# Token sums and reciprocals moved behind two groups of the output projection, and a third side unit moved ahead of the attention output

## The chip, the cores and the metric

The kernel runs on one core of one Trainium2 chip. Its time is the device time of that core in microseconds (us). A comparison goes by the median of several runs of each kernel on the same chip. Beside the timed runs there is one execution that the hardware profiler recorded; busy times, waits and starts of single instructions come from it.

## The reference

The inputs are a sequence of 2048 tokens of width 512, cut into 64 segments of 32 tokens, and a memory of 8 rows. Two branches are mixed by a gate for each token:

```
g = sigmoid((x * gate_w).sum(-1))
out = g * A(x) + (1 - g) * B(x)

A: for each segment s, in order
   h = [mem (8 rows), segment (32 rows)]
   q, k, v = h @ Wq, h @ Wk, h @ Wv          # 32 heads of width 128
   p = softmax(q k^T * scale, masked)        # memory columns are always open
   o = (p v) @ Wo
   mem = o[:8]                               # needed by the next segment
   result rows = o[8:]
B: layernorm -> @ w1 -> gelu -> @ w2
```

The 64 segments form a chain: the memory that segment s hands over is 8 rows of its output projection, and nothing of q, k and v of segment s+1 is complete without it. Branch B does not depend on the chain.

## The kernel before

**Stages.** A first stage of about 80 us computes branch B for part of the tokens and loads the four weight matrices. Then a loop of 64 steps follows, one for each segment. The kernel writes out the order of every engine's instructions by hand (`tc.manual_schedule()`), so the order in the source is the order on each engine. `T, si = divmod(s, 4)`: four segments make one tile of 128 tokens.

**The 32 columns of a step.** A step works on 8 memory rows and 24 of its own 32 tokens. The last 8 tokens of each segment ("left" tokens) are collected for a whole tile. Their q, k, v (`left_qk`, `left_v`) and their output projection (`wo_left`) are computed as filling work, called side units here: generators, from which `run(n)` takes the next n units. One unit is four matmuls with 512 moving columns each, which run side by side on four column tiles of TensorE (in tile 15 it is eight matmuls of 256 columns of branch B). `side(T, si)` picks the generator, and `WS` says how many units are taken at three places: `W1` before the attention output, `W2` between it and the output projection, `W3` after the projection.

**One step on TensorE, in order.**
1. `qk_unit` (L128): q and k of the step, 16 groups of four matmuls. ScalarE casts each bank (L133), VectorE transposes it into `QT` and `KT` (L137).
2. `scores(s, 0)` (L266, L270) for the first half of the heads, then v of the first half (`v_unit`, L147) and the first quarter of the second.
3. `xsums(E, 0)` (L702): the sums of the exponentials over the keys for the token queries, as eight tiny matmuls (4 moving columns, the exponentials as weights) into eight columns `xs8` of the bank `SbF`. Then `msum(0)` (L277, L280): the same for the memory queries, which `mnorm(0)` (L799, L800 on VectorE) turns into normalised weights in `E`.
4. `scores(s, 1)`, the rest of v, `msum(1)` and `mnorm(1)`, and two halves of a matmul unit of branch B (L675). `v_cast` (L809) copies v to SBUF on ScalarE.
5. `run(W1)`, then `xsums(E, 1)` and `recip_x(s)`.
6. `av` (L290, L295): the attention output of all heads, on four row tiles, first for heads of the first half and then of the second. The second half needs the result of `mnorm(1)`.
7. ScalarE copies the memory columns to `UT` (L840, four copies) and the token columns unnormalised to `XR` (L708, `x_raw`). Meanwhile `run(W2)`.
8. `wo_pass` (L159): the output projection as 8 groups of four matmuls of 512 columns into bank `X2`. The weights are `UT`: 8 memory columns of this step and 24 token columns of the step before, so the tokens lag one step.
9. `new_mem` (L747): the 8 memory rows are transposed into `hT` of the next step, with units of `W3` between.

**The token normalisation.** `recip_x` takes the reciprocal of `xs8` on VectorE (L713), stores it to DRAM (`r_dr`, L716 on the SP queue), issues the next load of `hm` (L654), and reads `r_dr` back as `Rb`, the same values on all partitions (L719, 512 KB written). VectorE then copies two results (L721) and writes the mask for the next step into `SbF`, which also clears `xs8` (`mask_put(0)`, L259); GpSimd adds to `racc` (L723). In the next step `x_norm` (L731) multiplies `XR` by `Rb` on GpSimd: two operations into `UT`, two into `UL`. `wo_pass` of that next step reads this `UT`. `prep_q` (L249) and `prep_h` (L245) stand in GpSimd's queue as well.

The lines that the change touches, with their surroundings:

Of the kernel before, what the change touches and what calls it, by code (L numbers as in the profile page):

```python
# [28 lines left out]
def kernel(ctx, tc, A_x, A_mem0, A_Wq, A_Wk, A_Wv, A_Wo, A_seg_len, B_x, B_w1, B_b1, B_w2, B_b2, gate_w, out):  # L29
    nc = tc.nc  # L30
    P = 128
    _, S, Dm = A_x.shape
# [80 lines left out]
    X2 = lps.tile([P, 512], FP32)  # L113
    SbF = lps.tile([P, 512], FP32)
    W = lps.tile([P, 512], FP32)
# [39 lines left out]
    def wo_group(bk, U_, n):  # L155
        j, ih = HORD[n]
        for c in range(4):
            i = 4 * ih + c
            nc.tensor.matmul(bk[32 * c:32 * c + 32, :], lhsT=U_[:, j, i, :], rhs=Wo_sb[:, 4 * i + j, :],  # L159
                             start=(n == 0), stop=(n == NW - 1), tile_position=(0, 32 * c))  # L160
# [6 lines left out]
    def flush(q, n=1):  # L167
        for _ in range(min(n, len(q))):
            q.pop(0)()
# [73 lines left out]
    def prep_h(s):  # L243
        T, si = divmod(s, SPT)
        nc.gpsimd.tensor_copy(out=hT[s % 3][:, :, 0:RIDE], in_=xTs[T][:, :, seg * si:seg * si + RIDE])  # L245
# [11 lines left out]
    def mask_put(i2):  # L257
        c = 4 * EW + (NG + 2 * M if i2 == 0 else 0)
        nc.vector.tensor_copy(out=(SbF, U[0])[i2][:, 0:c], in_=MkF[:, 0:c])  # L259
# [346 lines left out]
    UT = [lp.tile([P, 4, NG, 32], BF16, name=f"UT{i}") for i in range(2)]  # L606
# [22 lines left out]
    def side(T, si):  # L629
        gens = []  # L630
        if si == 2:
            gens = [wo_left(T - 1, X1) if T >= 1 else mlp_units(8)]
        elif T + 1 == NT:
            gens = [mlp_units(4)] if si < 2 else []
        else:
            gens = [[left_qk(T + 1, 0, 0, X1), left_qk(T + 1, 1, 0, U[3])], [left_qk(T + 1, 0, 1, X1), left_qk(T + 1, 1, 1, U[3])], [],
                    [left_v(T + 1, 0, X1), left_v(T + 1, 1, U[3])]][si]
        return chain(*gens)
# [10 lines left out]
    def hm_load(n):  # L649
        for _ in range(n):  # L650
            if work:
                T, fc = work.pop(0)
                hm = cw.tile([P, P], BF16, tag="hm", bufs=5, name="hm")
                nc.sync.dma_start(hm[:], h_dr[T][fc])  # L654
                hms.append((T, fc, hm, 1))
# [42 lines left out]
    def xsums(E, h):  # L698

        for c0, n in ((8, 32), (0, LEFT)):  # L700
            for c in range(4):
                nc.tensor.matmul(xs8[32 * c:32 * c + n, 4 * h:4 * h + 4], lhsT=E[:, 4 * h + c, c0:c0 + n], rhs=BO[:, 0:P:32],  # L702
                                 start=False, stop=True, skip_group_check=True, tile_position=(0, 32 * c))
# [7 lines left out]
    def recip_x(s):  # L711
        R = Rs.pop(s)
        nc.vector.reciprocal(out=R[:, 8 * NG:RW], in_=xs8)  # L713

        Rb = cw.tile([P, P, NG], FP32, tag="Rb", bufs=1, name="Rb")
        nc.sync.dma_start(r_dr[s % 2][:], R[:, 8 * NG:RW])  # L716
        hm_load(owed[0])
        owed[0] = 0
        nc.sync.dma_start(Rb[:].rearrange("p r e -> p (r e)"), r_dr[s % 2][:].rearrange("r e -> (r e)").partition_broadcast(P))  # L719
        for i2 in (1, 0):  # L720
            nc.vector.tensor_copy(out=R[:, 32 * i2:32 * i2 + 32], in_=RP[i2])  # L721
        mask_put(0)
        nc.gpsimd.tensor_tensor(out=racc[:, 0:RW], in0=racc[:, 0:RW], in1=R[:, 0:RW], op=ALU.add)  # L723
        Rbs[s] = Rb

    def x_norm(s):
        T, si = divmod(s, SPT)
        XR, Rb = XRs.pop(s), Rbs.pop(s)[:].rearrange("p (c q) (h j) -> p h j c q", c=4, h=2)
        for out, o, a, b in ((UT[(s + 1) % 2], M, LEFT, 32), (UL[T % 2], LEFT * si, 0, LEFT)):
            for h in range(2):  # L730
                nc.gpsimd.tensor_tensor(out=out[:, :, 4 * h:4 * h + 4, o:o + b - a], in0=XR[:, :, 4 * h:4 * h + 4, a:b], in1=Rb[:, h, :, :, a:b], op=ALU.mult)  # L731

    def wo_pass(U_, cuts=(0, Dm), bk=W):
        for n in range(NW):
            wo_group(bk, U_, n)
        w = cw.tile([P, Dm], BF16, tag="w", bufs=8, name="w")
        for a, b in zip(cuts, cuts[1:]):
            nc.scalar.copy(out=w[:, a:b], in_=bk[:, a:b])  # L738
        return w
# [9 lines left out]
        nc.vector.tensor_copy(out=hn[:, k0:k0 + nk, RIDE:32], in_=bk.rearrange("p (k m) -> p k m", k=nk))  # L749


    WS = ((2, 2, 1), (2, 2, 2), (2, 2, 2), (2, 2, 2))
    for s in range(nseg):
        T, si = divmod(s, SPT)
        last = s == nseg - 1
        hc, hn = hT[s % 3], hT[(s + 1) % 3]
        W1, W2, W3 = WS[si]
        fill = side(T, si)
        if s + 1 < nseg:
            prep_h(s + 1)  # L760
        if s >= 1:
            x_norm(s - 1)
        if si == 0 and T >= 2:
            c_load(T - 2)
        if si < 3:
            vp_load(T, si + 1)
        if last:
            c_load(T - 1)
            c_load(T)
        if si == 0 and T + 2 < NT:  # L770
            load_xT(T + 2)
        if s in (2, (NT - 1) * SPT):
            hm_load4()
        for n, (t, hf) in enumerate(((0, 0), (1, 0), (0, 1), (1, 1))):
            bk = U[n]
            for kc in range(KC):
                qk_unit(bk, hc, t, hf, kc)
            if n == 0:
                flush(act_q, 9)
                flush(dve_q, 9)  # L780
            qk_tr(qk_cast(bk[:]), (QT, KT)[t], hf, LEFT * (1 - t))
            if n == 0:
                mask_put(1)
        V = cw.tile([P, NG, Dh], BF16, tag="V", name="V")
        E = cw.tile([P, NG, EW], BF16, tag="E", name="E")
        R = cw.tile([P, NG * 40], FP32, tag="R", name="R")
        Rs[s] = R
        xsum = SbF[:, 0:32 * NG].rearrange("p (i q) -> p i q", q=32)

        def exps(i2, x):  # L790
            c = slice(0, 40) if x else slice(40, EW)
            nc.scalar.activation(out=E[:, 4 * i2:4 * i2 + 4, c], in_=Sb[i2][:, :, c], func=ACTF.Exp, scale=scale)  # L792

        def msum(i2):
            sums(U[1 + 2 * i2][:, 320:352].rearrange("p (i q) -> p i q", q=8), E[:, 4 * i2:4 * i2 + 4, :], 40, 48, 8, True)

        def mnorm(i2):
            r, e = RP[i2], E[:, 4 * i2:4 * i2 + 4, 40:56].rearrange("p i (a q) -> p i a q", q=8)
            nc.vector.reciprocal(out=r, in_=U[1 + 2 * i2][:, 320:352])  # L799
            nc.vector.tensor_tensor(out=e, in0=e, in1=r.rearrange("p (i q) -> p i q", q=8).unsqueeze(2).to_broadcast([P, 4, 2, 8]), op=ALU.mult)  # L800

        scores(s, 0)
        nc.scalar.activation(out=E[:, 0:4, :], in_=Sb[0], func=ACTF.Exp, scale=scale)
        for kc in range(KC):
            v_unit(X1, hc, 0, kc)

        def v_cast(vb, h):
            i0 = 4 * vb + 2 * h
            nc.scalar.copy(out=V[:, i0:i0 + 2, :].rearrange("p i e -> p (i e)"), in_=(X1, X2)[vb][:, 256 * h:256 * h + 256])  # L809

        v_cast(0, 0)
        v_unit(X2, hc, 1, 0)
        if not last:
            xsums(E, 0)
            msum(0)
            mnorm(0)
        scores(s, 1)
        exps(1, 0)
        v_cast(0, 1)
        exps(1, 1)  # L820
        for kc in range(1, KC - 1):
            v_unit(X2, hc, 1, kc)
        if not last:
            if s:
                next(mlp, None)
            msum(1)
            mnorm(1)
        v_unit(X2, hc, 1, KC - 1)
        for h in range(2):
            v_cast(1, h)  # L830
        if last:
            break
        run(W1)
        if s:
            next(mlp, None)
        xsums(E, 1)
        recip_x(s)
        av(s, V, E)
        for j in (0, 2, 1, 3):
            nc.scalar.copy(out=UT[s % 2][:, j, :, 0:M], in_=U[j][:, 0:NG * 40].rearrange("p (i q) -> p i q", q=40)[:, :, 32:40])  # L840
        x_raw(s)
        run(W2)
        prep_q(s + 1)
        w = wo_pass(UT[s % 2], (0, P, 2 * P, Dm), X2)
        if s >= 1:
            ws[s - 1] = w
        run(W3)
        for _ in extra(T, si):
            pass
        new_mem(w, hn, 0)  # L850
        run(1)
        new_mem(w, hn, 1)
        run(1)
        new_mem(w, hn, 2)
        for _ in fill:
            pass
        if si == 3 and T + 2 < NT:
            left_x(T + 2)
        flush(dve_q, 9)
        nc.vector.tensor_tensor(out=rmin[:, 0:RW], in0=rmin[:, 0:RW], in1=R[:, 0:RW], op=ALU.min)  # L860
        flush(act_q, 9)
# [174 lines left out]
```

## Time and profile before

| what | value |
|---|---|
| median of 3 runs | 759.48 us (759.0 to 761.15) |
| the profiled execution, its own time | 762.61 us |
| its span | 760.8 us, TensorE clock 0.999 |
| TensorE matmul busy | 741.7 us, 97% |
| ScalarE busy | 537.2 us, 71% |
| VectorE busy | 400.5 us, 53% |
| GpSimd busy | 274.7 us, 36% |

In the rows of the trace the engines are PE (TensorE matmuls), PEld (its weight loads), DVE (VectorE), ACT (ScalarE), POOL (GpSimd) and SPq (the queue of SyncE that issues DMAs). A row of the timeline gives start, duration, engine, line, operation, tiles with their shapes, and in brackets the idle time of the engine before it with what ended it. Consecutive instructions of one kind are merged (x8), and their duration is then from the first start to the last end. A matmul's duration contains the way through the array, so the distance between the starts of two groups is the better measure of what a group costs: the groups of four 512-column matmuls follow each other every 0.21 us, though one is listed with 0.38 us. For the same reason a TensorE that is busy 97% of the time is not without waits.

### The profile page before, as it was taken

Reading aid. Unit: us, or ns where it says so; the run is one execution under the profiler, and the core shown is the slowest. Engines: PE = TensorE matmul, PEld = TensorE weight load, DVE = VectorE, ACT = ScalarE, POOL = GpSimd, SP = SyncE. Lnnn points to the kernel's source line nnn. Section 1 sums busy time; section 2 is a strip of 40 time slices with the busy share of each in tenths; the row PEclk is TensorE's granted clock in tenths of the full one; section 3 lists DMA queues with packets and bytes.
Section 4 is the critical chain, followed back from the end, with each engine's and each line's share of the span. In section 5 each row is a group of like instructions: output and inputs, shape, how many; then the busy total and the mean of one; then the engine's idle time right before and its main releaser. Section 6 shows DMA issues by size and latency. Waiting matters only on the chain.

```text
span 760.8 us, 44957 instructions
## 1 busy us (share of the span) xinstructions
PE 741.7 (97%) x19710; PEld 422.9 (56%) x19710; DVE 400.5 (53%) x1415; ACT 537.2 (71%) x1626; POOL 274.7 (36%) x517
## 2 busy tenths in 40 slices
PE   8999999999999999999999999999999999999996
PEld 4776455555555555555555556555555555555553
DVE  5767545545445545446454555444454545545454
ACT  5767666777777777777777777677777777777663
POOL 4001234433344342443434443424433344442441
PEclk9999999999999999999999999999999999999999
DMA  9999522232222323122222213232222212222221
GB/s 308 324 319 332 136 75 60 69 83 78 66 64 72 94 66 90 59 74 76 80 80 63 87 47 99 66 86 56 73 77 90 79 61 72 61 87 73 85 69 45
DMA packets 74971, 75.70 MB, mean 99 GB/s; under 512 B 42377, under 2 KB 64882, under 8 KB 73234
## 3 DMA queue, kind: packets, MB, share of 16 engines
q1 hardware_dynamic: 73730, 71.07, 30.9%
q8 instruction: 156, 2.56, 1.4%
q0 software_dynamic: 496, 1.18, 0.5%
q10 hardware_dynamic: 544, 0.52, 0.2%
q14 instruction: 45, 0.37, 0.2%
HBM read 59.49 MB, written 6.98 MB: 87 GB/s over the span
## 4 chain that ended last, share of the span: by engine, by line
PE 86%; issue 1%; DVE 1%; ACT 0%; DVEq 0%; POOL 0%
PE U L128 33%; PE X L159 18%; PE X L147 16%; PE X L128 4%; PE U L290 3%; PE W L675 2%; PE U L147 2%; PE U L266 1%; PE U L747 1%; PE SbF L266 1%; PE U L295 1%; PE SbF L702 1%; PE U L277 1%; PE W L159 0%; PE U L280 0%
## 5 line engine op out<-in xcount | busy, mean ns | idle before, releaser
L731 POOL TENSOR_TENSOR UT<-XR,Rb 128x384 bf16<-128x384 bf16 x126 | 140.1, 1134 | 309.2 <-DMA Rb<-r_dr 261.2
L133 ACT CAST Tb<-U 128x512 bf16<-128x512 f32 x288 | 168.9, 587 | 81.6 <-PE U L128 79.0
L128 PEld LDWEIGHTS <-hT 128*32 128x32 bf16 x4096 | 107.8, 96 | 100.3 <-DVE hT L749 8.1
L147 PE MATMUL X<-Wv_sb,hT 128*32 128x512 bf16 x2048 | 144.6, 378 | 0.5 <-issue 0.5
L128 PE MATMUL U<-Wq_sb,hT 128*32 128x512 bf16 x2048 | 136.5, 381 | 0.2 <-DVE hT L749 0.2
L128 PE MATMUL U<-Wk_sb,hT 128*32 128x512 bf16 x2048 | 133.2, 379 | 0.0
L159 PE MATMUL X<-Wo_sb,UT 128*32 128x512 bf16 x2016 | 121.0, 380 | 0.2 <-issue 0.2
L749 DVE CAST hT<-U 128x8 bf16<-128x8 f32 x126 | 21.0, 167 | 167.6 <-PE U L747 126.5
L809 ACT CAST V<-X 128x256 bf16<-128x256 f32 x256 | 88.7, 372 | 15.7 <-PE X L147 5.0
L137 DVE STREAM_TRANSPOSE QT<-Tb 128x256 f32<-128x256 f32 x128 | 56.6, 442 | 73.7 <-ACT Tb L133 73.0
L159 PEld LDWEIGHTS <-UT 128*32 128x32 bf16 x2080 | 57.1, 96 | 56.1 <-issue 14.0
L708 ACT CAST XR<-U 128x256 bf16<-128x256 f32 x252 | 78.3, 432 | 0.0
L738 ACT CAST w<-X 128x128 bf16<-128x128 f32 x189 | 44.7, 309 | 44.8 <-PE X L159 44.8
L137 DVE STREAM_TRANSPOSE KT<-Tb 128x256 f32<-128x256 f32 x128 | 56.9, 445 | 30.9 <-ACT Tb L133 23.2
L731 POOL TENSOR_TENSOR UL<-XR,Rb 128x128 bf16<-128x128 bf16 x126 | 60.3, 501 | 0.0
L147 PEld LDWEIGHTS <-hT 128*32 128x32 bf16 x2048 | 47.1, 95 | 21.6 <-issue 1.0
L840 ACT CAST UT<-U 128x64 bf16<-128x64 f32 x252 | 35.9, 225 | 28.3 <-PE U L295 28.3
L723 POOL TENSOR_TENSOR racc<-racc,R 128x72 f32<-128x72 f32 x63 | 21.2, 337 | 94.7 <-DVE R L721 81.8
L792 ACT ACTIVATE E<-U 128x64 bf16<-128x64 f32 (+1 forms) x128 | 35.0, 273 | 11.4 <-PE U L270 10.8
L480 PEld LDWEIGHTS <-w_sb 128*128 128x128 bf16 (+1 forms) x352 | 33.5, 100 | 15.2 <-issue 2.4
L747 PEld LDWEIGHTS <-w 128*32 128x32 bf16 x1008 | 23.6, 93 | 31.9 <-ACT w L738 25.2
L128 PE MATMUL X<-Wq_sb,GL 128*32 128x512 bf16 x496 | 38.7, 381 | 1.3 <-issue 1.2
(173 smaller groups left out, 1237.8 us busy)
## 6 DMA issues: line engine op xcount, KB each, us to landing
Rb<-r_dr SPq DMA_DIRECT2D x63, 512.0 KB, 4.0
Wv_sb<-in_A_Wv_dram SPq DMA_DIRECT2D x4, 1024.0 KB, 6.5
Wq_sb<-in_A_Wq_dram SPq DMA_DIRECT2D x4, 1024.0 KB, 8.5
Wk_sb<-in_A_Wk_dram SPq DMA_DIRECT2D x4, 1024.0 KB, 8.5
Wo_sb<-in_A_Wo_dram SPq DMA_DIRECT2D x4, 1024.0 KB, 11.3
VP<-VL SPq DMA_DIRECT2D x64, 64.0 KB, 3.5
hm<-h_dr SPq DMA_DIRECT2D x69, 32.0 KB, 2.0
c<-c_dr SPq DMA_DIRECT2D x16, 128.0 KB, 3.5
```

The lines of the kernel that those rows point to most:

```text
L128: nc.tensor.matmul(bk[32 * j:32 * j + 32, :], lhsT=G[:, kc, :], rhs=W5[t][:, kc, h0:h1, j, :], start=(kc == 0), stop=(kc == KC - 1), tile_ ...
L133: nc.scalar.copy(out=Tb[:], in_=bk.rearrange("p (a b e) -> p a e b", a=8, b=2))
L137: nc.vector.transpose(out=dst[:, 8 * hf:8 * hf + 8, c0:c0 + 32, :].rearrange("p a r b -> p a (r b)").bitcast(FP32), in_=Tb[:].rearrange("p ...
L147: nc.tensor.matmul(bk[32 * j:32 * j + 32, :], lhsT=G[:, kc, :], rhs=Wv5[:, kc, 4 * vb:4 * vb + 4, j, :], start=(kc == 0), stop=(kc == KC - ...
L159: nc.tensor.matmul(bk[32 * c:32 * c + 32, :], lhsT=U_[:, j, i, :], rhs=Wo_sb[:, 4 * i + j, :], start=(n == 0), stop=(n == NW - 1), tile_po ...
L480: nc.tensor.matmul(hp[:rows, 0:TB * P], lhsT=w1_sb[:, kc, fc * P:fc * P + rows], rhs=yTs[blk][:, kc, :], start=(kc == 0), stop=(kc == KC - 1))
L708: nc.scalar.copy(out=XR[:, j], in_=U[j][:, 0:NG * 40].rearrange("p (i q) -> p i q", q=40)[:, :, 0:32])
L731: nc.gpsimd.tensor_tensor(out=out[:, :, 4 * h:4 * h + 4, o:o + b - a], in0=XR[:, :, 4 * h:4 * h + 4, a:b], in1=Rb[:, h, :, :, a:b], op=ALU ...
L738: nc.scalar.copy(out=w[:, a:b], in_=bk[:, a:b])
L792: nc.scalar.activation(out=E[:, 4 * i2:4 * i2 + 4, c], in_=Sb[i2][:, :, c], func=ACTF.Exp, scale=scale)
L809: nc.scalar.copy(out=V[:, i0:i0 + 2, :].rearrange("p i e -> p (i e)"), in_=(X1, X2)[vb][:, 256 * h:256 * h + 256])
L840: nc.scalar.copy(out=UT[s % 2][:, j, :, 0:M], in_=U[j][:, 0:NG * 40].rearrange("p (i q) -> p i q", q=40)[:, :, 32:40])
```

## The change

Three edits. The two `xsums` calls and `recip_x` leave their places before `av` and are handed to `wo_pass` as a function `mid`, which is called after the second of its eight groups; so both `xsums` run there one after the other, 16 tiny matmuls, followed by all that `recip_x` issues. `WS` takes three side units before the attention output and one after it, in place of two and two; the number after the projection stays. On VectorE, ScalarE and the SP queue the order of instructions stays as it was, apart from single places in the last tile; on GpSimd `prep_q` now stands before the addition to `racc`.

```diff
-    def wo_pass(U_, cuts=(0, Dm), bk=W):
+    def wo_pass(U_, cuts=(0, Dm), bk=W, mid=None):
         for n in range(NW):
             wo_group(bk, U_, n)
+            if n == 1 and mid:
+                mid()
@@
-    WS = ((2, 2, 1), (2, 2, 2), (2, 2, 2), (2, 2, 2))
+    WS = ((3, 1, 1), (3, 1, 2), (3, 1, 2), (3, 1, 2))
@@
         if not last:
-            xsums(E, 0)
             msum(0)
             mnorm(0)
@@
         run(W1)
         if s:
             next(mlp, None)
-        xsums(E, 1)
-        recip_x(s)
         av(s, V, E)
...
         run(W2)
         prep_q(s + 1)
-        w = wo_pass(UT[s % 2], (0, P, 2 * P, Dm), X2)
+
+        def token_sums():
+            for h in range(2):
+                xsums(E, h)
+            recip_x(s)
+
+        w = wo_pass(UT[s % 2], (0, P, 2 * P, Dm), X2, token_sums)
```

## The prediction

> **What bounds the kernel now.** I read the page's head and the groups first, then how regular the steps are, then the timeline of one undisturbed step around the moved work, and last the steps that are longer.
>
> ```profile
> span 760.8 us, 44957 instructions
> PE 741.7 (97%) x19710; PEld 422.9 (56%) x19710; DVE 400.5 (53%) x1415; ACT 537.2 (71%) x1626; POOL 274.7 (36%) x517
> ...
> PE 86%; issue 1%; DVE 1%; ACT 0%; DVEq 0%; POOL 0%
> ```
>
> TensorE bounds the whole span, and no single wait stands out. So the change can win or lose only in the small waits of a step. The reciprocal of the token sums (L713) runs once a step, so its starts give the length of steps:
>
> ```profile
> L713 DVE RECIPROCAL R<-SbF x63: 195/208/208, 87.5 to 738.1; 128x8 f32<-128x8 f32 x63
> ...
> 360.86 0.21 DVE L713 RECIPROCAL R<-SbF 128x8 f32<-128x8 f32 x1 [0.21 <-PE SbF L702]
> 371.09 0.21 DVE L713 RECIPROCAL R<-SbF 128x8 f32<-128x8 f32 x1 [0.22 <-PE SbF L702]
> ...
> 423.08 0.21 DVE L713 RECIPROCAL R<-SbF 128x8 f32<-128x8 f32 x1 [0.21 <-PE SbF L702]
> 433.54 0.21 DVE L713 RECIPROCAL R<-SbF 128x8 f32<-128x8 f32 x1 [0.21 <-PE SbF L702]
> ```
>
> A clean step takes 371.09 - 360.86 = 10.23 us; where `out_sel` runs as well (14 steps) it takes 10.46. From 87.5 to 738.1 are 62 steps, 650.6 us. Clean they would take 62 x 10.23 + 14 x 0.23 = 637.5. So 13.1 us are irregular waits, and the rest is a fixed chain that repeats. I take it apart in the step around 412 us:
>
> ```profile
> 410.47 0.45 DVE L137 STREAM_TRANSPOSE KT<-Tb 128x256 f32<-128x256 f32 x1 [0.36 <-ACT Tb L133]
> 410.83 0.20 PE L702 MATMUL SbF<-BO,E 128*32 128x4 bf16 x8
> 410.89 0.18 PE L277 MATMUL U<-E,BO 128*32 128x32 bf16 x4
> 410.96 0.18 PEld L266 LDWEIGHTS <-KT 128*32 128x32 bf16 x16
> ...
> 411.93 0.61 PE L147 MATMUL X<-Wv_sb,GL 128*32 128x512 bf16 x8
> 412.16 0.65 ACT L809 CAST V<-X 128x256 bf16<-128x256 f32 x2
> 412.36 0.29 PE L675 MATMUL W<-w_sb,hm 128*32 128x256 bf16 x4
> 412.41 0.23 DVE L800 TENSOR_TENSOR E<-E,RS 128x64 bf16<-128x64 bf16 x1
> 412.47 0.22 PE L702 MATMUL SbF<-BO,E 128*32 128x4 bf16 x8
> 412.62 0.27 PE L290 MATMUL U<-E,V 32*128 32x40 bf16 x16
> 412.76 0.32 PE L290 MATMUL U<-E,V 32*128 32x40 bf16 x16
> 412.85 0.21 DVE L713 RECIPROCAL R<-SbF 128x8 f32<-128x8 f32 x1 [0.22 <-PE SbF L702]
> 412.93 0.19 PE L295 MATMUL U<-E,VP 32*128 32x64 bf16 x4
> 413.05 0.62 PE L147 MATMUL X<-Wv_sb,GL 128*32 128x512 bf16 x8
> 413.15 0.56 ACT L840 CAST UT<-U 128x64 bf16<-128x64 f32 x4 [0.35 <-PE U L295]
> 413.48 0.15 PEld L159 LDWEIGHTS <-UT 128*32 128x32 bf16 x8 [0.31 <-issue]
> 413.51 0.40 PE L159 MATMUL X<-Wo_sb,UT 128*32 128x512 bf16 x4
> ```
>
> Two things are to be seen. The second scores load `KT` at 410.96, 0.04 us after its transpose ends (410.47 + 0.45): their start belongs to VectorE. And after the attention output's last group (412.93) two side units run from 413.05 on, and two take 0.43 (411.93 to 412.36, where the next work starts), so until 413.48; the projection's weights load at 413.48, after the ScalarE copy that started at 413.15 and that a wait of 0.31 us on the load queue stands for. Two units cover the copy of `UT` almost exactly, with nothing to spare.
>
> **The change part by part.** The sum is made against the profiled execution, 762.6 us, which lies 3.1 above the median of the runs shown, 759.5; the difference is carried over to that median. The moved work issues in 63 steps.
>
> *Side unit ahead of the attention output.* A unit costs 0.43/2, rounded 0.21 us of TensorE. Put before `av`, it delays all that follows by that. Behind `av` nothing is saved: the first projection group starts 413.51 - 412.93 = 0.58 us after `av`'s last group whatever stands between, since L295, then the copy L840, then the weight load is the chain. With one unit TensorE is done at about 413.26 on this step's clock and waits 0.25. The cover that was used there is gone, and what is late next is the projection and with it the new memory. Bounds: 0 (if something before `av` held TensorE that long) and +0.21; the rows from 411 on show full groups up to 412.36, so +0.21.
>
> *`xsums(E, 1)` out of the place before `av`.* Between L675 and `av` lie 0.26 us now (412.36 to 412.62): 0.11 for 256 columns, 0.06 for the eight tiny matmuls, 0.09 for the change from column to row tiles, which stays. Bounds 0 and -0.06; I take -0.04.
>
> *Waits within `av`.* Its second half waits for `v_cast`, which ends at 412.81 (412.16 + 0.65). With `av` 0.17 later this wait goes. From 412.76 to 412.93 are 0.17, and the first half takes 0.14 for as many matmuls: bounds 0 and -0.04, and I take -0.025.
>
> *`xsums(E, 0)` out of the place before `msum(0)`.* The eight cost 0.06 us there (410.83 to 410.89), but what follows waits for `KT` at 410.96 anyway. Gain: 0. Only the wait grows.
>
> *Both inside the projection.* 16 tiny matmuls between groups of 512 columns, at the 0.06 for eight just read: +0.11 (bounds 0.06, if the first eight hide behind the group ahead, and 0.20, with a bubble like the 0.09 above). Nothing hides it: the copies of `w`, `new_mem` and the next step's q hang on the projection's last group.
>
> *What `recip_x` issues.* L713, two L721 and L259 take 0.8 us on VectorE (412.85 to 413.65) and would end some 1.2 us before the copies for `hT` that stand behind them: 0. The store, the load of `hm` and the load of `Rb` keep their order on SP; `hm` has several tiles in flight: 0. On GpSimd `racc` and `prep_q` swap places: 0.
>
> Fixed part: 0.21 - 0.04 - 0.025 + 0.11 = +0.26 us a step, times 63 = **+16.4 us**.
>
> *The token normalisation comes later.* L713 now follows `av` (0.28), the gap (0.58), two groups (0.43) and the way from the first sum to VectorE (0.38 for eight, 412.47 to 412.85, and 0.06 for the others): 1.7 us after `av`'s start against 0.23 now, 1.5 later. The chain behind it:
>
> ```profile
> 391.79 0.21 DVE L713 RECIPROCAL R<-SbF 128x8 f32<-128x8 f32 x1 [0.22 <-PE SbF L702]
> 398.92 1.13 POOL L731 TENSOR_TENSOR UT<-XR,Rb 128x384 bf16<-128x384 bf16 x1 [5.72 <-ACT Tb L133]
> 401.11 0.95 POOL L731 TENSOR_TENSOR UL<-XR,Rb 128x128 bf16<-128x128 bf16 x2
> 401.58 0.56 DVE L800 TENSOR_TENSOR E<-E,RS 128x64 bf16<-128x64 bf16 x1
> 401.80 0.27 PE L290 MATMUL U<-E,V 32*128 32x40 bf16 x16
> 402.07 0.20 DVE L713 RECIPROCAL R<-SbF 128x8 f32<-128x8 f32 x1
> 402.20 0.28 PE L290 MATMUL U<-E,V 32*128 32x40 bf16 x16
> 407.48 1.13 POOL L731 TENSOR_TENSOR UT<-XR,Rb 128x384 bf16<-128x384 bf16 x1 [4.03 <-DMA Rb<-r_dr]
> ...
> L800 DVE TENSOR_TENSOR E<-E,RS x63: 224/226/893, 87.2 to 737.8; 128x64 bf16<-128x64 bf16 x63
> ```
>
> `x_norm` starts 5.4 us (402.07 to 407.48) to 7.1 us (391.79 to 398.92) after L713 and occupies GpSimd for 3.1 us. While it does, the L800 with both inputs in SBUF (`E`, `RS`) is held: it took 0.56 us and ended at 402.14, after GpSimd's 402.06, and `av`'s second half came 0.40 after the first instead of 0.14. Its longest is 0.893 against 0.226. Counted from `av`'s start, `x_norm` now runs from 5.6-7.3 to 8.8-10.5, and L800 comes at 10.0, so only the latest collide, and I put them at 1.5 us in all. Afterwards `x_norm` runs from 7.1-8.8 to 10.2-11.9 and L800 comes at 10.1: nearly every step collides. L800 gained 0.17 of slack from the side unit and has about 0.4 in all, so the short operations on `UL` (0.5) hardly matter; one on `UT` (1.13) leaves 0 to 0.7. Some 45% of the steps fall there (`x_norm` starting after 7.9), at a mean of 0.22: 63 x 0.45 x 0.22 = 6.2, and 1.1 for the few steps where the DMA is so late that the projection waits for `UT`. Against 1.5 now: **+5.8 us** (bounds -1.5 and +9).
>
> The Trainium skill, "SBUF — State Buffer", section "SBUF: two separate sides", says that VectorE with two SBUF inputs and GpSimd take a port pair exclusively for a whole instruction; it speaks against moving GpSimd's work onto L800, and the trace agrees, with 0.893 against 0.226.
>
> *The irregular waits.* The 13.1 us less 1.5 leave about 11.6 in steps like this one:
>
> ```profile
> PE U L295 <- issue: 3.1, 6, 0.8
> ...
> 210.66:213.62 2.96, 2.96 (x138) 1.95 (x131) 1.83 (x7) 2.43 (x8) 1.52 (x3) 1.00 0.36 76
> 205.30:210.66 5.36, 5.36 (x133) 2.68 (x128) 2.14 (x8) 3.57 (x9) 1.64 (x2) 1.00 0.47 137
> ...
> 213.61 0.19 PE L295 MATMUL U<-E,VP 32*128 32x64 bf16 x2
> 214.64 0.20 PE L295 MATMUL U<-E,VP 32*128 32x64 bf16 x2 [0.84 <-issue]
> ...
> q8 instruction: 156, 2.56, 1.4%
> ```
>
> TensorE stops in the middle of four like matmuls, with no semaphore. Queue q8 brings instructions in pieces of 2.56 MB / 156 = 16 KB, about 256 of TensorE's 39420 loads and matmuls (128 pairs). Six such stops fall on L295 alone (the waits' row), others close by; they come every third step, when a block that starts near the first scores ends at `av`: its 128 pairs (138 with those over the edges) ran in 2.96 us, against 5.36 for the block before, which ended without a stop. The next piece, I infer, is there only some 3.5 to 4 us after the last. The change takes 32 rows of tiny sums out of that stretch and puts 8 of a side unit in, so the same block ends 24 rows further, behind `av`, the remaining unit, the wait for `UT` and two groups of the projection. That is about 0.9 us later, as much as the longest of these stops. I leave 2 of the 11.6 us: **-9.6 us** (bounds 0 and -11.6).
>
> The Trainium skill, "Runtime: NRT & Kernel Launch", section "Instruction fetch mechanics", has blocks of 256 instructions too, but calls the crossing mostly hidden. By that there would be nothing to win here; the 0.84 us of idle before 214.64 says otherwise, and the measurement decides.
>
> Sum: 16.4 + 5.8 - 9.6 = +12.6 us; 762.6 becomes 775.2, and at the runs' median 759.5 + 12.6 = **772 us**, slower by 1.7%. A difference within 0.3% (2.3 us) can't be told from no change.
>
> **The rivals.**
> - *Faster: the side unit falls into a wait.* If the head of `av` is held by `mnorm(1)` or `v_cast` for 0.21 us or more a step, the unit is free. Then 772 - 63 x 0.21 = 759, and without collisions 753. For it: the second half of `av` does wait for `v_cast`. Against: it does so by less than 0.06, and `av`'s first matmul follows the last tiny sum by no more than the change of tiles takes. It decides from 0.20 us of wait a step on (12.6/63). 6%.
> - *Collisions in every step.* If L800 meets the first half of a `UT` operation each time, as in its longest case, `av` waits 0.45 us more: 63 x 0.45 = 28 in place of 7.3, 793 us. For it: the windows overlap in nearly all steps. Against: the DMA's time scatters by 1.7 us. 8%.
> - *No collisions*, because VectorE gets in between two operations or `Rb` lands sooner: 772 - 7.3 = 765. 18%.
> - *The instruction blocks go on stopping TensorE*, at another place: 772 + 9.6 = 782. For it: as many instructions in a step as before, and 16 tiny ones in one place make a new fast stretch. Against: it is followed and preceded by groups of 0.21 us for eight rows. 12%. If the 11.6 us come from something else than the blocks, nothing is won either, and the time is the same. By the page of the Trainium skill named last ("Runtime: NRT & Kernel Launch", "Instruction fetch mechanics") it would come out so.
>
> **How the numbers follow.** My forecast has 56%; with it, the rival without collisions and the one at 782 it is slower by over 0.3%, and so is the 793. Slower: 56 + 18 + 12 + 8 = 94, less 4 that I keep for an edit mispriced in the fixed part: 90%. Of these 4 and the 6 of the first rival, 7 are faster and 3 within 0.3%. The range goes from 764 (no collisions, the stops gone wholly) to 782 (the stops unchanged).
>
> **What the profile after would show.** PEld's wait before the first L159 of a step grows to about 0.5 us, and one group of L147 or L128 lies between L295 and L159. A clean step takes 10.49 us. L266's second load stays 0.04 us behind `KT`'s transpose. The median of L800 on `RS` rises well above 226 ns, with `x_norm` ending near or behind `av`'s start. Idle of TensorE put down to "issue" around L295 falls. Wrong would be: a clean step of 10.3 or less, or the first L159 within 0.4 us of the last L295.

## The result and the profile after

The changed kernel takes 782.27 us (median of 4 runs, 781.26 to 783.25), the kernel before 759.24 (median of 4, 758.42 to 761.15): a ratio of 1.0294, 95% interval 1.0271 to 1.0318. It is slower, as forecast, by 23.0 us where 12.6 were forecast, and it lies 0.3 us above the range's upper end. The profiled execution of after took 783.25 us, 1.0 above its median; that of before lay 3.4 above its own. So 2.4 of the 23.0 us don't stand between the two traces, whose spans differ by 20.6 us.

The page's head and the shares of the chain, after:

```profile
span 781.4 us, 44943 instructions
PE 756.4 (97%) x19710; PEld 422.9 (54%) x19710; DVE 417.1 (53%) x1415; ACT 536.6 (69%) x1626; POOL 273.6 (35%) x517
...
PE 84%; DVE 5%; DMA 4%; ACT 3%; issue 2%; POOL 1%; SPq 0%; DVEq 0%; POOLq 0%; ACTq 0%
```

TensorE has as many instructions as before. VectorE's busy time grew by 16.6 us (400.5 to 417.1) with as many instructions, and its share of the chain went from 1% to 5%: the first sign of an operation that is held. A clean step, in the timeline:

```profile
369.15 0.28 PE L290 MATMUL U<-E,V 32*128 32x40 bf16 x16
...
377.33 0.45 DVE L137 STREAM_TRANSPOSE KT<-Tb 128x256 f32<-128x256 f32 x1 [0.36 <-ACT Tb L133]
...
377.83 0.17 PEld L266 LDWEIGHTS <-KT 128*32 128x32 bf16 x16
...
379.65 0.27 PE L290 MATMUL U<-E,V 32*128 32x40 bf16 x16
379.79 0.28 PE L290 MATMUL U<-E,V 32*128 32x40 bf16 x16
379.89 0.22 PE L295 MATMUL U<-E,VP 32*128 32x64 bf16 x4
380.05 0.40 PE L147 MATMUL X<-Wv_sb,GL 128*32 128x512 bf16 x4
380.17 0.56 ACT L839 CAST UT<-U 128x64 bf16<-128x64 f32 x4 [0.52 <-PE U L295]
380.50 0.24 PEld L159 LDWEIGHTS <-UT 128*32 128x32 bf16 x8 [0.35 <-issue]
380.53 0.62 PE L159 MATMUL X<-Wo_sb,UT 128*32 128x512 bf16 x8
380.96 0.27 PE L702 MATMUL SbF<-BO,E 128*32 128x4 bf16 x16
381.04 0.57 PEld L159 LDWEIGHTS <-UT 128*32 128x32 bf16 x16
381.38 0.21 DVE L713 RECIPROCAL R<-SbF 128x8 f32<-128x8 f32 x1 [1.79 <-PE SbF L702]
```

From one `av` to the next are 379.65 - 369.15 = 10.50 us; 10.49 was forecast, against 10.23 before. The second scores' weights load 0.05 us after `KT`'s transpose ends (377.83 against 377.78). One group lies between L295 and the projection, and the projection starts 0.64 us after L295's last group, as long as before to within 0.06: TensorE waits for the copy of `UT` instead of covering it.

The waits of TensorE and of its loads (sum in us, times, longest); all but the second are new or have grown:

```profile
PEld L290 <- issue: 17.8, 56, 0.6
PEld L159 <- issue: 15.4, 45, 0.3
PEld L290 <- DVE E L802: 7.7, 24, 0.4
PEld L159 <- POOL UT L731: 3.7, 8, 1.0
PEld L675 <- DMA hm<-h_dr: 2.5, 1, 2.5
PEld L159 <- POOL UL L871: 1.9, 1, 1.9
...
PE U L290 <- DVE E L802: 3.0, 10, 0.5
```

L802 is the old L800, which finishes `mnorm`. The 17.8 and 7.7 us in the load queue before `av` are not a sign that it is held. The loads of `av`'s first half wait there in the clean step above too, where TensorE works on L675 meanwhile, and the wait is put down to L802 although nothing is held:

```profile
379.42 0.29 PE L675 MATMUL W<-w_sb,hm 128*32 128x256 bf16 x4
379.64 0.17 PEld L290 LDWEIGHTS <-V 32*128 32x128 bf16 x16 [0.32 <-DVE E L802]
```

What the hold costs is therefore read from the starts of `av`'s two halves. The group of L802, with the least, median and longest duration in ns:

```profile
L802 DVE TENSOR_TENSOR E<-E,RS x63: 225/435/1151, 86.5 to 756.9; 128x64 bf16<-128x64 bf16 x63
```

And the timeline of a step in which it is held (L731 is `x_norm`):

```profile
388.58 2.18 POOL L731 TENSOR_TENSOR UT<-XR,Rb 128x384 bf16<-128x384 bf16 x2 [5.88 <-ACT V L811]
389.76 1.08 DVE L802 TENSOR_TENSOR E<-E,RS 128x64 bf16<-128x64 bf16 x1
390.13 0.24 PE L290 MATMUL U<-E,V 32*128 32x40 bf16 x11
390.61 0.21 PE L290 MATMUL U<-E,V 32*128 32x40 bf16 x5 [0.23 <-issue]
390.71 0.94 POOL L731 TENSOR_TENSOR UL<-XR,Rb 128x128 bf16<-128x128 bf16 x2
390.89 0.28 PE L290 MATMUL U<-E,V 32*128 32x40 bf16 x16
```

Its median doubled, 226 to 435 ns. Here it came while GpSimd's second operation on `UT` ran and ended at 390.84, 0.08 us after that; `av`'s second half began at 390.89, 0.76 after the first instead of 0.14. The stop of 0.23 us at 390.61 lies within this wait.

Three other waits stand beside these. TensorE waits 2.36 us for `hm` in one step, whose load is now issued later; in two steps, of which one is shown, the projection waits for a late `UT`; and TensorE still stops with no semaphore:

```profile
111.01 2.95 SPq L654 DMA_DIRECT2D hm<-h_dr  x4
112.20 0.18 PE L749 MATMUL U<-SelM,w 128*32 128x8 bf16 x4
114.73 0.40 PE L675 MATMUL W<-w_sb,hm 128*32 128x256 bf16 x8 [2.36 <-DMA hm<-h_dr]
...
132.29 2.16 POOL L731 TENSOR_TENSOR UT<-XR,Rb 128x384 bf16<-128x384 bf16 x2 [7.52 <-ACT V L811]
134.50 0.40 PE L159 MATMUL X<-Wo_sb,UT 128*32 128x512 bf16 x4 [0.66 <-POOL UT L731]
...
270.30 0.20 PE L270 MATMUL U<-QT,KL 128*32 128x64 bf16 x4
270.95 0.62 PE L147 MATMUL X<-Wv_sb,hT 128*32 128x512 bf16 x8 [0.45 <-issue]
```

To add this up I cut every step of both traces at the starts of the same matmuls (q, first and second scores, `av`, last L295, projection, new memory) and took each piece's median over the steps. What a piece is longer than its median is its irregular part.

| piece | before, us | after, us | difference | forecast |
|---|---|---|---|---|
| second scores to `av` | 1.650 | 1.812 | +0.162 | +0.17 |
| within `av` | 0.316 | 0.278 | -0.038 | -0.025 |
| last L295 to the projection | 0.574 | 0.602 | +0.028 | 0 |
| projection | 1.531 | 1.636 | +0.105 | +0.11 |
| others | | | 0 | 0 |
| step | | | +0.257 | +0.26 |

| irregular, us over 62 steps | before | after |
|---|---|---|
| `av`'s second half waits for a held L800/L802 | 1.2 | 7.9 |
| projection waits for a late `UT` (two steps) | 0 | 1.7 |
| TensorE waits for `hm` (one step) | 0 | 2.5 |
| stops of TensorE without a semaphore and what is left | 12.1 | 5.1 |
| sum | 13.3 | 17.2 |

In some steps of before `av` has both a held L800 and a stop. The step of the prediction's example is one: near the end of its `av`, three matmuls start 0.40 us after the one ahead of them:

```profile
402.30 0.18 PE L295 MATMUL U<-E,VP 32*128 32x64 bf16 x1
402.70 0.21 PE L295 MATMUL U<-E,VP 32*128 32x64 bf16 x3 [0.21 <-issue]
```

Only the delay up to the start of the second half counts as held.

62 x 0.257 = 15.9, with 3.9 of irregular waits 19.8; the loop's measured growth is 19.5 (651.5 to 671.0 from the first q to the last). The remaining 1.1 of 20.6 lie outside the loop, where the projection behind the last step waits 1.9 us on the load queue for `UL` (L871), a row that before doesn't have.

### The profile page after: what moved, and what is told of

Read it like the earlier page. It is cut to its first block, busy times and chain, and to the rows that moved or that the text cites. A ratio compares the mean times of both kernels' runs of the same rounds, so it can differ in the third digit from the quotient of the medians.

```text
span 781.4 us, 44943 instructions
## 1 busy us (share of the span) xinstructions
PE 756.4 (97%) x19710; PEld 422.9 (54%) x19710; DVE 417.1 (53%) x1415; ACT 536.6 (69%) x1626; POOL 273.6 (35%) x517
## 4 chain that ended last, share of the span: by engine, by line
PE 84%; DVE 5%; DMA 4%; ACT 3%; issue 2%; POOL 1%; SPq 0%; DVEq 0%; POOLq 0%; ACTq 0%
PE U L128 31%; PE X L159 18%; PE X L147 15%; PE U L290 3%; ACT UT L839 2%; PE X L128 2%; DVE E L802 2%; PE U L487 2%; PE W L675 2%; PE U L147 2%; PE U L266 2%; PE SbF L480 1%; DMA Rb<-r_dr 1%; PE W L480 1%; DMA w_sb<-in_B_w_dram 1%
## 5 line engine op out<-in xcount | busy, mean ns | idle before, releaser
L731 POOL TENSOR_TENSOR UT<-XR,Rb 128x384 bf16<-128x384 bf16 x126 | 139.5, 1130 | 341.4 <-DMA Rb<-r_dr 183.1
L128 PEld LDWEIGHTS <-hT 128*32 128x32 bf16 x4096 | 106.3, 96 | 102.7 <-DVE hT L751 9.8
L159 PE MATMUL X<-Wo_sb,UT 128*32 128x512 bf16 x2016 | 127.7, 379 | 6.2 <-POOL UT L731 1.6
L159 PEld LDWEIGHTS <-UT 128*32 128x32 bf16 x2080 | 50.9, 95 | 50.5 <-issue 15.4
L713 DVE RECIPROCAL R<-SbF 128x8 f32<-128x8 f32 x63 | 13.1, 208 | 103.8 <-PE SbF L702 101.8
L731 POOL TENSOR_TENSOR UL<-XR,Rb 128x128 bf16<-128x128 bf16 x126 | 60.0, 499 | 0.0
L751 DVE CAST hT<-U 128x8 bf16<-128x8 f32 x126 | 20.9, 166 | 72.8 <-PE U L749 50.9
L147 PEld LDWEIGHTS <-hT 128*32 128x32 bf16 x2048 | 46.6, 95 | 23.3 <-issue 2.4
L675 PE MATMUL W<-w_sb,hm 128*32 128x256 bf16 x552 | 39.6, 273 | 2.4 <-DMA hm<-h_dr 2.4
## 6 DMA issues: line engine op xcount, KB each, us to landing
Wo_sb<-in_A_Wo_dram SPq DMA_DIRECT2D x4, 1024.0 KB, 11.2
```

The source lines that it names most:

```text
L128: nc.tensor.matmul(bk[32 * j:32 * j + 32, :], lhsT=G[:, kc, :], rhs=W5[t][:, kc, h0:h1, j, :], start=(kc == 0), stop=(kc == KC - 1), tile_ ...
L147: nc.tensor.matmul(bk[32 * j:32 * j + 32, :], lhsT=G[:, kc, :], rhs=Wv5[:, kc, 4 * vb:4 * vb + 4, j, :], start=(kc == 0), stop=(kc == KC - ...
L675: nc.tensor.matmul(W[32 * c:32 * c + 32, cc], lhsT=hm[:, 32 * c:32 * c + 32], rhs=w2_sb[:, fc, cc], start=(fc == 0 and h == 0), stop=(fc = ...
```

## The experiments

The theory on trial was the prediction's: a fixed cost of 0.26 us a step, of which 0.21 comes from the unit; collisions of `x_norm` with the VectorE operation with two SBUF inputs; and stops that depend on where blocks of instructions end. The later kernels test what the first left open.

**The unit alone.** Before, with only:

```diff
-    WS = ((2, 2, 1), (2, 2, 2), (2, 2, 2), (2, 2, 2))
+    WS = ((3, 1, 1), (3, 1, 2), (3, 1, 2), (3, 1, 2))
```

> The third side unit ahead of the attention output, the sums and the reciprocal at their old places. Theory (the unit is added to the chain because the copy of UT takes its time whatever fills it): a clean step of 10.43 to 10.44 us, that is 63 x 0.20 = +12.9 us, less some 4 us of block waits and collisions (a block that ended at the attention output now ends 8 rows further, L800 has 0.2 us more slack): 768 us. Rival (the unit falls into a wait ahead of the attention output): a clean step of 10.25 or less and 757 to 760 us.

Measured: 767.33 us against 757.58 for before on the same chip, 1.0127 (1.0081 to 1.0172). L713 follows `xsums(E, 1)` in this kernel, so its starts give the step:

```profile
363.56 0.21 DVE L713 RECIPROCAL R<-SbF 128x8 f32<-128x8 f32 x1 [0.43 <-PE SbF L702]
374.00 0.21 DVE L713 RECIPROCAL R<-SbF 128x8 f32<-128x8 f32 x1 [0.43 <-PE SbF L702]
384.44 0.21 DVE L713 RECIPROCAL R<-SbF 128x8 f32<-128x8 f32 x1 [0.43 <-PE SbF L702]
```

A step of 10.44 us: 0.21 above 10.23. By pieces, second scores to `av` grew by 0.213, `av` shrank by 0.037, the way to the projection grew by 0.028. The rival that the unit falls into a wait is refuted: it is paid in full, and behind `av` nothing comes back. 63 x 0.21 = 13.2, yet the kernel is only 9.8 us slower, so by the times some 3.4 us of irregular waits are gone, though this edit leaves the tiny sums where they were. Between the two profiled executions they fell by more, from 13.3 to 6.4 us; that of before is 3.4 us slower than its median.

**The sums alone.** After, with `WS` as before:

```diff
-    WS = ((3, 1, 1), (3, 1, 2), (3, 1, 2), (3, 1, 2))
+    WS = ((2, 2, 1), (2, 2, 2), (2, 2, 2), (2, 2, 2))
```

> The sums and the reciprocal inside the projection, two side units on each side as before. Theory: a clean step of 10.33 us (the wait for v stays, 0.10 more in the projection), +6.6 us; L800 collides with x_norm in most steps as in the changed kernel but without the 0.2 us of slack from the unit, +12 to +17 us; block waits around the attention output mostly gone, -6 us: 770 to 776 us. Rival (the unit alone is the loss, the token sums cost nothing where they stand): 756 to 761 us.

Measured: 774.83 against 757.58, 1.0226 (1.0183 to 1.0268), within the expected 770 to 776. The fixed pieces are nearly free: second scores to `av` 1.597 us (-0.053), projection 1.636 (+0.105). The rest is the held operation:

```profile
L802 DVE TENSOR_TENSOR E<-E,RS x63: 225/426/1156, 86.3 to 749.3; 128x64 bf16<-128x64 bf16 x63
```

It is held no longer than in after (median 426 ns against 435), but without the unit `av` comes sooner and has no slack: its waits for L802 sum to about 15.5 us, against 7.9 in after. The unit, a loss by itself, hid half of this.

**After, without the collisions.** The reciprocal goes to a PSUM bank, so that L802 has only one input in SBUF:

```diff
-    RP = [SbF[:, 288:320], RS[:]]
+    RP = [SbF[:, 288:320], SbF[:, 320:352]]
```

> The changed kernel, but the reciprocal of the second half of the memory sums lies in PSUM (columns 320 to 352 of SbF) in place of SBUF, so that L800 no longer reads two inputs from SBUF; the computation is the same. Theory (GpSimd holds exactly that operation): no L800 over 0.25 us, the attention output loses its 7.9 us of waits, 782 - 8 = 774 us. Rival (L800 is late for another reason, or the time is the DMA's): L800 stays long in some 25 steps and the time stays at 780 to 783 us.

Measured: 776.62 against 757.58, 1.0236 (1.0183 to 1.0288); 774 was expected. The operation, now in all 126 cases with one input in PSUM:

```profile
L802 DVE TENSOR_TENSOR E<-E,SbF x126: 220/221/223, 86.4 to 748.8; 128x64 bf16<-128x64 bf16 x126
```

It is never held, though `x_norm` stands where it stood, and waits of `av` for it sum to 0.2 us. The irregular sum fell from 17.2 to 8.8. So the collision is shown to be the cause of those 7.9 us, and the two inputs in SBUF to be its condition. The Trainium skill's page "SBUF — State Buffer", section "SBUF: two separate sides", gives that condition; 223 ns at most here against 1151 agrees. By time alone the gain (1.0294 to 1.0236) isn't certain, since the intervals overlap.

**After, with `hm` loaded as early as before.** The one wait of 2.36 us was not in the sum, so I tried its cause:

```diff
+        hm_load(owed[0])
+        owed[0] = 0
         av(s, V, E)
```

> The changed kernel, but the loads of hm are issued ahead of the attention output as before the change, and the store and reload of the reciprocals stay where the change puts them. Theory (in the step where branch B takes eight units, late hm loads stop TensorE once for 2.4 us): that wait at L675 is gone, 779.8 us. Rival (it is a single late DMA of the profiled execution): no change, 782 us.

Measured: 778.37 against 757.58, 1.0285 (1.0239 to 1.0332). The time alone can't tell this from 1.0294. The trace can: of L675's waits on the load queue that for `hm` is gone, and only this is left:

```profile
PEld L675 <- issue: 1.1, 2, 0.7
```

The piece from the new memory to the next q lost its 2.5 us. It was the place of the load on the SP queue, behind the later store: all four kernels that load `hm` inside the projection (after, the sums alone, and these two with the reciprocal in PSUM) have this wait once, and the other nine have none. It is longest in after, 2.5 us on the load queue, and 0.6 to 0.8 us in the other three.

**Before, with the stops moved.** If the stops depend on where blocks end, then instructions added ahead of the loop move them. Eight (and in another kernel 24) matmuls of 4 columns whose result nobody reads follow the first ones of the program, each with a weight load:

```diff
         warm(NWARM)
+        for _ in range(8):
+            nc.tensor.matmul(U[3][:, 0:4], lhsT=ident[:], rhs=ident[:, 0:4], start=True, stop=True, skip_group_check=True)
```

> The kernel before with 8 tiny matmuls (4 columns, on constants, result unused) added on TensorE in the first stage where it waits for inputs: with their loads 16 more instructions ahead of the loop, so that all blocks of 256 instructions end 16 instructions earlier in the loop's work. Theory (TensorE stops where a block is used up faster than the next one is fetched): the stops inside the attention output lose more than half, 10 us of block waits become about 5, 4 to 6 us faster than before. Rival (the stops belong to the attention output, whatever the blocks): same stops at the same places, time within 0.3%.

> As the run with 8, but 24 tiny matmuls, 48 instructions. Theory: the block ends fall another 32 instructions earlier, ahead of the attention output but still within the fast stretch, and the stops come back there: 0 to 2 us faster than before. Rival: within 0.3%, stops as before.

Measured: 762.01 and 762.97 against 761.16, 1.0013 (0.9992 to 1.0033) and 1.0019 (1.0003 to 1.0035). No gain by time. The fixed pieces are those of before, and the irregular sums of the profiled executions are 10.1 and 12.2 us against 13.3. But with 24 the stops went elsewhere; the waits of the projection's loads sum to 22.7 us in 67, in the view of waits, where before has 15.6 in 47:

```profile
PEld L159 <- issue: 22.7, 67, 0.9
```

Three of the longest, in the timeline:

```profile
109.81 0.97 PEld L159 LDWEIGHTS <-UT 128*32 128x32 bf16 x21 [0.88 <-issue]
...
423.44 0.77 PEld L159 LDWEIGHTS <-UT 128*32 128x32 bf16 x20 [0.62 <-issue]
...
487.63 0.98 PEld L159 LDWEIGHTS <-UT 128*32 128x32 bf16 x23 [0.79 <-issue]
```

In 16 steps, three apart mostly (2, 5, 8, ... 59), the projection is 0.1 to 0.8 us longer, 5.3 us in all, where before it had 0.9; the stops at `av` became fewer in turn. 48 instructions far ahead of the loop moved the stops within the step, which a semaphore, a DMA of the kernel or another engine would not explain. So the stops go with the count of instructions.

The traces show this more directly when TensorE's loads, its matmuls and the few instructions of its sequencer are numbered in order. I took every gap of over 0.33 us between the starts of two matmuls, between 84 and 745 us, that has no releaser ("issue"). In the 13 profiled executions there are 113, of them 15 in before and 5 in after, and all stand at the same number within a block of 256: at 192 or 193 in six kernels, at 172 or 173 in the other seven. Each ends 1.2 to 1.6 us after a piece of 16 KB on q8 has landed. So the stops are shown to belong to the blocks of 256 instructions; that it is the next piece they wait for is read from these times alone. The stops at this number sum to 12.2 us in the loop of before, 4.8 in after, and 8.4 and 11.1 with 8 and 24 matmuls. With the times unchanged, that moving them takes them away is refuted.

**Before, without collisions.** The same edit of `RP` as above, in before, alone and with the eight matmuls:

```diff
-    RP = [SbF[:, 288:320], RS[:]]
+    RP = [SbF[:, 288:320], SbF[:, 320:352]]
```

> The kernel before with the reciprocal of the second half of the memory sums in PSUM in place of SBUF. Theory: no L800 over 0.25 us (12 were, the longest 0.893), 1.5 to 3 us faster. Rival (those steps wait for instructions anyway): no L800 over 0.25 us and no change of the time.

> Both edits, the reciprocal in PSUM and 8 tiny matmuls, on the kernel before. Theory: they add up, 5 to 9 us faster than before, 749 to 753 us where before takes 758. Rival (the waits take each other's place): 2 to 4 us.

Measured: 769.18 and 771.14 against 761.16, 1.0100 (1.0080 to 1.0119) and 1.0127 (1.0104 to 1.0150). Both expectations missed; the edit makes before slower. The timeline of the first of them, and its waits:

```profile
371.77 0.22 DVE L800 TENSOR_TENSOR E<-E,SbF 128x64 bf16<-128x64 bf16 x1
372.05 0.22 PE L702 MATMUL SbF<-BO,E 128*32 128x4 bf16 x8
372.05 0.11 PEld L702 LDWEIGHTS <-E 128*32 128x32 bf16 x7 [0.27 <-issue]
```

```profile
PEld L702 <- issue: 17.9, 63, 0.7
PE SbF L702 <- DVE E L800: 1.2, 4, 0.4
```

`xsums(E, 1)` writes other columns of the bank `SbF` in which the reciprocal now lies. It starts 0.06 us after L800 has read it (371.77 + 0.22 = 371.99), in each of 63 steps, 17.9 us in all; the way from second scores to `av` is 1.902 us instead of 1.650. The view names L800 as the releaser in four steps; in the others it is read from these ends. In the kernels with the sums behind `av` this order costs nothing. The irregular sums fell to 4.0 and 3.3 us.

**The sums alone, without collisions.** The sums-alone kernel with the edit of `RP`:

```diff
-    RP = [SbF[:, 288:320], RS[:]]
+    RP = [SbF[:, 288:320], SbF[:, 320:352]]
```

> Sums and reciprocal inside the projection, two side units on each side, and the reciprocal of the memory sums in PSUM. Theory (with the units left alone, what that version loses is nearly all collisions of L800 with x_norm): the 16.6 us of waits in the attention output go, no L800 over 0.25 us, a clean step of 10.33 to 10.34 us, 1.0226 becomes 1.000 to 1.006. Rival (the sums cost time in the projection beyond what the steps show): 1.015 or more.

Measured: 770.93 against 760.5, 1.0122 (1.0091 to 1.0154), above the expected 1.000 to 1.006 and below the rival's 1.015. The fixed pieces sum to +0.088 us a step (-0.053 to `av`, +0.037 in `av`, which waits for v again, +0.104 in the projection), 5.5 us. The irregular waits without the one for v are 13.3, as before: they did not fall here, which the expectation had counted on. The stops at block ends, 5.6 us with the sums alone, are 11.2 here. The last projection waits 2.6 us for `UL`. These give 8.1 of the 9.3 us that the ratio means; the rest is open.

**A smaller move.** Before, with `xsums(E, 1)` and `recip_x` only moved directly behind `av`, and the edit of `RP`:

```diff
-        xsums(E, 1)
-        recip_x(s)
         av(s, V, E)
+        xsums(E, 1)
+        recip_x(s)
```

> The kernel before, with only the second half of the token sums and all that recip_x issues moved behind the attention output, ahead of its copies, and the reciprocal of the memory sums in PSUM; units as before. Theory: the sums lie where TensorE waits for the copy of UT anyway, so a clean step is 10.23 to 10.27 us, no L800 is held, and 3 us of collisions go: 0.995 to 1.001. Rival (the wait for L800 that the PSUM version of the kernel before had comes back elsewhere): 1.008 or more.

Measured: 761.08 against 760.5, 1.0004 (0.9982 to 1.0025): no difference, as expected.

```profile
390.73 0.21 DVE L713 RECIPROCAL R<-SbF 128x8 f32<-128x8 f32 x1 [0.73 <-PE SbF L702]
400.99 0.21 DVE L713 RECIPROCAL R<-SbF 128x8 f32<-128x8 f32 x1 [0.72 <-PE SbF L702]
411.25 0.21 DVE L713 RECIPROCAL R<-SbF 128x8 f32<-128x8 f32 x1 [0.71 <-PE SbF L702]
```

A step takes 10.26 us. What the tiny sums save ahead of `av` (1.617 for 1.650) is given back within it (0.350 for 0.316), and the way to the projection grows by 0.037. Of all variants it is the best, and it only equals before.

**After, with both repairs.** The edits of `RP` and of `hm` in after:

```diff
-    RP = [SbF[:, 288:320], RS[:]]
+    RP = [SbF[:, 288:320], SbF[:, 320:352]]
...
+        hm_load(owed[0])
+        owed[0] = 0
         av(s, V, E)
```

> The changed kernel with both repairs, the reciprocal in PSUM and the hm loads ahead of the attention output. Theory: what is left is the fixed part, 63 x 0.254 = 16 us, less some 5 us of block waits that the change saves and 3 us of collisions that the kernel before has: +8 to +14 us, 1.011 to 1.018. Rival (block waits unchanged by the change): +16 us or more, 1.021 and up.

Measured: 773.21 against 760.5, 1.0165 (1.0121 to 1.0209), within the theory's 1.011 to 1.018; the rival of unchanged stops, from 1.021 on, lies just outside the interval. Two repairs take 1.3% off the 2.9%. What is left is the fixed part, 62 x 0.257 = 15.9, less 13.3 - 8.8 = 4.5 of irregular waits: 11.4 in the loop, 1.5%.

## Why the prediction came out as it did

The sign was right and the time 10.3 us short. The fixed part and the mechanisms hold; several sizes were off, and one term was wrongly put at 0. By the prediction's own steps:

- **Fixed part, +16.4: right.** 0.257 us a step were measured where 0.26 were summed, each piece within 0.03. The unit is paid in full (the unit alone); `xsums(E, 0)` leaves nothing behind, since `KT`'s transpose still decides; the 16 sums cost 0.105 in the projection. The gap behind `av`, taken as unchanged, grew by 0.028.
- **The token normalisation later, +5.8: right in its mechanism, 2.6 too small.** The held L800 and late `UT` grew by (7.9 + 1.7) - 1.2 = 8.4 us. The 1.5 of before was about right; in after 24 steps waited 0.33 us on average where 28 at 0.22 were summed, and `UT` was late by 1.7 in place of 1.1. The experiment with one PSUM input shows the mechanism.
- **The irregular waits, -9.6: the term that was mis-sized.** They fell by about 7.0, from 12.1 to 5.1, between the two profiled executions, and probably by less between typical ones (see the last item). That the stops belong to blocks of 256 instructions was right. But the prediction followed one block's end from `av` to a place behind the projection, and the rest of its kind reappeared elsewhere: after has them in 14 steps between second scores and `av`, as at 270.95. Nor was it the edit that the step named: the unit alone took the irregular waits from 13.3 to 6.4, the sums without collisions left them at 13.3. What goes with the smaller stops in all kernels is the longer step (last section).
- **"`hm` has several tiles in flight: 0": wrong, +2.5.** One step early in the loop waits 2.36 us for it, and the early load takes that away. The DMA that moves with `recip_x` was named, but its cover was asserted and not looked up.
- **The end of the kernel**, not in the sum: 1.1 us. The last `x_norm` has no next step to lie in. Some of this may be chance: the two padded kernels, with the order of before, also wait for this `UL`, 1.2 and 1.0 us.
- **The profiled execution**, 3.1 above the median of the runs shown and 3.4 above that of all: carried over as if after had the same, it had 1.0. This is the other 2.4. Behind the last q, before takes 29.3 us, no more than the unit alone and the padded kernels (28.8 to 31.9), so its surplus probably lies in its stops. Their fall would then be some 4.6 us between typical executions; this is not shown.

With these: 62 x 0.257 = 15.9, + 8.4 - 7.0 + 2.5 + 1.1 = 20.9, and 2.4 more is 23.3 against 23.0 measured. Two small sums of the prediction are off by a little over 1 us: the lower end of its range, 772 - 7.3 - 2, is 763 and not 764, and its first rival without collisions, 759 - 7.3, is 752 and not 753. Neither changes the account.

Of the rivals, the unit in a wait is refuted, no collisions too. Collisions in every step came closer than its 8%: L802 was held at its median, but most of that fell in the slack of 0.4 us, and about 24 of 63 steps cost something. The rival that stops go on unchanged gave the right time, 782, for the wrong reason: they did fall, and other waits filled the sum. The Trainium skill, "Runtime: NRT & Kernel Launch", section "Instruction fetch mechanics", which calls the crossing mostly hidden, would have given that time as well; the stop of 0.45 us before 270.95 and the 12.2 us of stops at block ends in before don't agree with it.

Of the signs named, the clean step (10.49), the place of L266, the one group, and the median of L800 came as said. The wait on the load queue before the first L159 was to grow to 0.5 us and is 0.35: the one unit's loads also wait until the array takes them, so the sum of this row (15.6 before, 15.4 after) shows nothing of the 0.27 us in which TensorE is idle (380.05 + 0.21 to 380.53). Idle by "issue" before L295 (3.1 us before) has no row any more.

## What to carry to other kernels

Work that covers a wait is not free to be moved ahead of the wait: it is paid where it goes, and the wait stays; here 0.21 us in each of 63 steps. When a step that issues DMAs moves, follow each transfer to the engine that uses it, and its last reader to every VectorE operation with two SBUF inputs that it may now meet while GpSimd runs; one input in PSUM ends that, if no matmul has to write the same bank meanwhile. Small stops of a full TensorE that no semaphore explains should not be counted as won because code moves past one of them: here moving the code moved them, and they were smaller only where the step was longer.

## What the runs showed of the hardware

- A VectorE operation with two SBUF inputs lasts until the running GpSimd operation ends: 225 ns undisturbed, up to 1151 ns here (1156 with the sums alone), ending 0.08 us after it at 390.84. With one input in PSUM it took 220 to 223 ns in 126 cases beside the same GpSimd work.
- The long stops of TensorE without a releaser all stand at one number within its blocks of 256 instructions (113 of 113). Over the loop the stops there sum to 8.3 to 12.2 us in the five kernels with a step of 10.23 to 10.32 us, and to 3.5 to 7.3 in the eight with 10.43 to 10.49, one execution each. That a slower step gives the next instructions time to arrive would fit, and is argued, not shown.
- A matmul into a PSUM bank started only after VectorE had read other columns of that bank, 0.25 us later a step. In four steps L800 is named as its releaser, which is inferred from a semaphore, so there the kernel's own dependency asks for it; whether the chip would as well was not tried.
